# Zero matmuls in TensorE's idle stretches at the start, all of batch 1 transposed on TensorE, and load limits in the kernel's own schedule

## The chip, the cores and the metric

The kernel runs on one core of a Trainium2 chip. The metric is device time in microseconds (us), the median of several executions of the whole program. The page of the profile is one execution, so its span differs a little from the median. PE is TensorE, DVE is VectorE, ACT is ScalarE, POOL is GpSimd and SP is SyncE. POOL starts nearly all loads. SP starts the first loads of q and k, the DMA transposes and the stores.

For one core, "slow" means that the run was more than 1.5% above the fastest of the same kernel. Ratios below use fast runs alone; medians and ranges are of all runs.

## The reference

Block-sparse attention feeds a linear "multiplicative" feed-forward layer (FFN). There are 4 batches of 8 heads, 768 positions and 64 dimensions per head.

```python
scores = q @ k.T / 8                               # per head
mask   = near | first block | last block | 3 sampled blocks per block of 32
attn   = softmax(where(mask, scores, -1e9)) @ v
x      = attn.transpose(0, 2, 1, 3).reshape(3072, 512)
out    = ((x @ w1) * (x @ w2)) @ w3 @ w_out        # 512 -> 1024 -> 1024 -> 512
```

## The kernel before

The kernel is a list of tasks, each with an estimated cost on each engine that may do it. A list scheduler inside the kernel simulates the five engines, decides the order, and emits the instructions in that order. Each engine then runs its own list strictly in that order. So a number in the simulation does not change any instruction. It changes who stands before whom, and an engine that meets an input that has not landed stands still, with everything behind it.

The parts that matter here are these (`...` marks cuts):

```python
PRM = dict(..., trb=6, ..., warm=0.0, nat=4, big=10)    # trb: pairs of heads transposed by PE

# Plan.run, the list scheduler
free.update({"PE": 0.9, "ACT": 2.1, "DVE": 0.9, "POOL": 1.25, "SP": 0.75})
...
if self.spare and free["PE"] < PRM["warm"]:             # warm = 0.0: never true
    ...                                                 # would insert one zero matmul
...
if t.kind == "load":
    from_ = max(lane, t.end + 1.75)
    lane = from_ + t.bytes / 375e3
    t.seen = lane + 0.2                                 # when the data is thought to land
elif t.kind == "xbar":                                  # DMA transposes
    ...
    t.seen = t.end + 1.6 + more
...
# one pair of heads: q and k have to be turned into head_dim x positions
if (b, pr) in by_pe:            # the first trb pairs: 12 PE transposes each for q and k, one PSUM copy each
    m = add("tr ...", {PE: 0.35 + SWITCH}, tr, deps=[LD[src], t_ident], ...)
    add("tc ...", both(0.81, 0.56), ...)                # ACT or DVE
else:                           # the others: DVE reorders into a "qs" buffer (4 of them), SP transposes by DMA
    m = add("re ...", {DVE: 0.37}, ..., writes=[("qs", b, pr, x)], ...)
    add("xb ...", {SP: 1.25}, dma_start(..., transpose=True), reads=[("qs", b, pr, x)], kind="xbar")
...
# attention output xn -> x, the FFN's input: also a DMA transpose on SP's queue
add("xx ...", {SP: 1.25}, dma_start(out=x, in_=xn, transpose=True), kind="xbar")
```

Batch 0 has four pairs and batch 1 has four. So `trb=6` sends the last two pairs of batch 1, and all of batches 2 and 3, through DVE and the DMA transposes.

The softmax here doesn't subtract the row's maximum and nothing guards it: scores larger than these inputs give would overflow.

Of the kernel before, what the change touches and what calls it, by code (L numbers as in the profile page):

```python
# [9 lines left out]
BF16 = mybir.dt.bfloat16  # L10
# [5 lines left out]
SEEN = {"PE": 0.22, "ACT": 0.10, "DVE": 0.10, "POOL": 0.12, "SP": 0.05}  # L16
# [6 lines left out]


PRM = dict(bias=0.4, bmask0=1.0, bmask=1.0, btc=0.5, near=0.12, soon=0.06, kprio=2.0, eprio=0.5, aprio=1.0,
           hprio=1.0, vprio=1.5, w3prio=10.0, ebufs=4, both=0.25, fo="31", pcopy=4.0, trb=6, units="tttt",
           warm=0.0, nat=4, big=10)
LONG = ("load", "xbar", "store")


# [10 lines left out]
class Plan:  # L41
# [12 lines left out]
    def add(self, name, costs, go, deps=(), writes=(), reads=(), kind="", prio=0, mode="N", flight=0.0, bias=None):  # L54
        t = Task(name, costs, [d for d in deps if d is not None], list(writes), list(reads), go,
                 kind, prio, mode, flight)
        t.bias = {"DVE": PRM["bias"]} if bias is None else bias
        for key in set(t.writes) | set(t.reads):
            self.users[key] += 1
        self.tasks.append(t)  # L60
        return t
# [32 lines left out]
    def run(self):  # L94
        waiting = {id(t): len(t.deps) for t in self.tasks}
        after = defaultdict(list)
        for t in self.tasks:
            for d in t.deps:
                after[id(d)].append(t)
        ready = [t for t in self.tasks if not waiting[id(t)]]  # L100
        free = defaultdict(float)
        free.update({"PE": 0.9, "ACT": 2.1, "DVE": 0.9, "POOL": 1.25, "SP": 0.75})
        lane = 0.0
        lanes = []
        mode = "N"
        self.log = []
        n = 0
        while ready:
            best = None
            ests = defaultdict(list)  # L110
            for t in ready:
                b = self.buffer_ready(t)
                if b is None:
                    continue
                base = b
                for eng in t.costs:
                    at = base
                    for d in t.deps:
                        at = max(at, d.end if d.eng == eng and not d.flight and d.kind not in LONG else d.seen)
                    t.base[eng] = max(at, free[eng])  # L120
                eng = min(t.costs, key=lambda e: t.base[e] + t.costs[e] + t.bias.get(e, 0.0))
                ests[eng].append((t.base[eng], t))
            if not ests:
                raise RuntimeError("stuck: " + " ".join(t.name for t in ready[:40]))
            picks = []
            for eng, cands in ests.items():
                if eng == "PE":
                    p = self.pick_pe(cands, free, mode)
                else:
                    p = self.pick(eng, cands, free)  # L130
                if p:
                    picks.append((p[0], eng, p[1]))
            if self.spare and free["PE"] < PRM["warm"]:
                pe = min([p[0] for p in picks if p[1] == "PE"], default=1e9)
                rest = min([p[0] for p in picks if p[1] != "PE"], default=1e9)
                if pe > free["PE"] + 0.2 and rest > free["PE"]:
                    w = self.spare(mode)
                    w.start, w.end, w.eng = free["PE"], free["PE"] + w.costs["PE"], "PE"
                    free["PE"] = w.end
                    self.log.append(w)  # L140
                    continue
            elif self.spare:
                self.spare = None
                self.left[("f", "warm")] = 0
                self.freed[("f", "warm")] = free["PE"] + SEEN["PE"]
            picks.sort(key=lambda p: (p[0], p[1]))
            start, eng, t = picks[0]
            if eng == "PE":
                if t.mode != mode:
                    start = max(start, free["PE"] + SWITCH)  # L150
                mode = t.mode
            self.commit(t, eng, start)
            free[eng] = t.end
            if t.kind == "load":
                from_ = max(lane, t.end + 1.75)
                lane = from_ + t.bytes / 375e3
                lanes.append((from_, lane, t.row))
                t.seen = lane + 0.2
                for key in t.writes:
                    self.freed[key] = t.seen  # L160
            elif t.kind == "xbar":
                busy = [row for a, z, row in lanes if a < t.start + 1.25 <= z]
                more = 4.0 * max(busy) / 4096 if busy else 0.0
                t.end = t.start + 1.25 + more
                free[eng] = t.end
                t.seen = t.end + 1.6 + more
                for key in set(t.writes) | set(t.reads):
                    self.freed[key] = max(self.freed[key], t.seen)
            elif t.kind == "store":
                for key in set(t.writes) | set(t.reads):  # L170
                    self.freed[key] = max(self.freed[key], t.end + 3.0)
            self.log.append(t)
            ready.remove(t)
            for u in after[id(t)]:
                waiting[id(u)] -= 1
                if not waiting[id(u)]:
                    ready.append(u)
            n += 1
        if n != len(self.tasks):
            raise RuntimeError("left over: " + " ".join(t.name for t in self.tasks if t.end is None)[:400])  # L180
        order = sorted(range(n), key=lambda i: (self.log[i].start, i))
        return self.log
# [35 lines left out]
def kernel(  # L218
# [12 lines left out]
    nc = tc.nc  # L231
# [12 lines left out]
    PE, ACT, DVE, POOL, SP = "PE", "ACT", "DVE", "POOL", "SP"  # L244
    both = lambda a, d: {ACT: a, DVE: d}
# [29 lines left out]
    def fixed(name, shape, dt):  # L275
        return const.tile(shape, dt, tag=name, name=name)
# [3 lines left out]
    def T(*key, shape=None, dt=None):  # L280
        if key[0] == "v1":
            return v1_all[:, (key[1] * NP + key[2]) % 8]
        if key not in tl:
            sh, ty, _, _ = spec[key[0]]
            tl[key] = pools[key[0]].tile(shape or sh, dt or ty, tag=key[0], name=key[0])
        return tl[key]

    plan = Plan({name: s[2] for name, s in spec.items()})
    add = plan.add
# [38 lines left out]
    def load(name, out_of, src, nbytes, writes, deps=()):  # L328
        seq[0] += 1
        t = add(name, {POOL: 0.73}, lambda t: nc.gpsimd.dma_start(out=out_of(), in_=src),  # L330
                deps=deps, writes=writes, kind="load", prio=seq[0])
        t.bytes = nbytes
        t.row = 1536 if name.startswith("ld") else 4096
        return t

# [8 lines left out]
    for nm, dst, src, at in (("qn", q32, qv, 4.0), ("kn", k32, kv, 5.0)):  # L344
        ld = add(f"first {nm}", {SP: 0.43}, lambda t, dst=dst, src=src: nc.sync.dma_start(
            out=dst, in_=src[0][:, 0:2]), prio=-2, flight=at - 1.2)
# [31 lines left out]
    for item in LOADS.split():  # L378
        kind, rest = item[0], item[1:]
# [8 lines left out]

    t_ones = add("ones", {DVE: 0.15}, lambda t: nc.vector.memset(
        v1_all[:, :, :, :, D:].rearrange("p a b c d -> p (a b c) d"), 1.0), prio=-1)  # L390
    zero = fixed("zero", [128, 512], BF16)
    t_zero = add("zero", {DVE: 0.2}, lambda t: nc.vector.memset(zero, 0.0), prio=-1)
    add("warm", {PE: 0.43}, lambda t: nc.tensor.matmul(
        T("f", "warm"), lhsT=zero[:, :128], rhs=zero, start=True, stop=True),
        deps=[t_zero], writes=[("f", "warm")], prio=-1)
    plan.users[("f", "warm")] += 1

    def spare(mode):
        rows = 64 if mode == "S" else 128
        return Task("spare", {PE: 0.11}, (), (), (), lambda t: nc.tensor.matmul(  # L400
            T("f", "warm")[:, :256], lhsT=zero[:rows, :128], rhs=zero[:rows, :256], start=True, stop=True),
            "spare", 0, mode, 0.0)
    plan.spare = spare

    def dve(name, cost, deps, go, **kw):
# [30 lines left out]
    for i, (lo, n) in enumerate(((0, 512), (512, 256))):  # L436
# [3 lines left out]
            deps=[t_Ab, t_hot], writes=[key], prio=2)  # L440
# [67 lines left out]
    units = []  # L508
# [11 lines left out]
    for m in range(len(tiles) // 2):  # L520
        ek = ("e", m)
        exps, masks = [], []
        for j, (b, t3, pr, kp) in enumerate(tiles[2 * m:2 * m + 2]):
            sk, qk = ("s", b, t3, pr, kp), ("qkt", b, pr)

            def sc(t, sk=sk, qk=qk, t3=t3, kp=kp):
# [12 lines left out]
                prio=PRM["eprio"]))  # L539
# [3 lines left out]
            deps=exps + [t_mask[t3, kp], t_mask[t3, kp + 1]], writes=[ek], prio=PRM["kprio"])  # L543
        for j, (b, t3, pr, kp) in enumerate(tiles[2 * m:2 * m + 2]):
# [14 lines left out]
            if kp < 2:  # L559
# [7 lines left out]
                deps=[tr], reads=[ok, rk], writes=[xk], prio=0)  # L567
# [4 lines left out]
    for b in range(B):  # L572
        for t3 in range(NT):
            xk = ("xn", b, t3)
            i, half = divmod(b * NT + t3, 2)
            for qt in range(2):
# [3 lines left out]
                    deps=Xdone[b, t3], writes=[("x", i)], reads=[xk], kind="xbar", prio=0)  # L580
# [33 lines left out]
    for i in range(NU):  # L614
        hk, xk = [("big", "h", i, j) for j in range(NF // 2)], ("x", i)
        hs = []
        for f in range(NF):
            ends = {}
            for which, w in (("w1", w1_sb), ("w2", w2_sb)):
                key = ("f", which, i, f)  # L620
                last = None
                for part in range(2):
                    def mm(t, key=key, w=w, f=f, part=part, xk=xk):
                        for c in range(2 * part, 2 * part + 2):
# [4 lines left out]
                               writes=[key], reads=[xk],  # L629
# [66 lines left out]
```

## Time and profile before

The median was 262.42 us in 3 runs (260.9 to 263.03).

| what | value | read from |
|---|---|---|
| span of the profiled run | 261.6 us | page |
| PE busy | 242.8 us, 93% | page, part 1 |
| first real PE work | 4.60 us | timeline |
| PE at half rate | until about 22.9 us | durations in the timeline |
| PE idle in 60-70 and 80-90 us | 2.9 and 3.2 us | windows |
| last value product (end of attention) | 222.4 us | groups by source line |

The profiled run itself took 263.41 us, a little more than the three, at a mean clock of 0.987.

The first view is the page: busy microseconds by engine, then the granted PE clock in 40 slices (tenths of full speed).

```profile
PE 242.8 (93%) x2555; PEld 128.5 (49%) x2597; DVE 175.2 (67%) x305; ACT 186.6 (71%) x231; POOL 44.6 (17%) x73
...
PEclk9999999998899979999999999999999999999999
```

PE is the limit. The clock row says "full speed" from the start, but the durations say otherwise. The next lines are the timeline of the opening: start, duration, engine, line of the kernel, operation, output<-inputs, shape and count, and in brackets the idle time before and what ended it. L477 is the transposes of q and k, L531 the scores.

```profile
4.60 0.85 PE L477 MATMUL f<-ident,qn 128*64 128x128 bf16 x12 [2.39 <-ACT qn L292]
8.59 1.03 PE L531 MATMUL s<-qkt 64*128 64x256 bf16 x8
...
20.22 0.54 POOL L330 DMA_DIRECT2D big<-in_moe_w_dram  x1 [1.65 <-DMA kn<-in_k_dram]
22.20 0.84 PE L477 MATMUL f<-ident,kn 128*64 128x128 bf16 x12 [0.36 <-issue]
23.94 0.61 PE L531 MATMUL s<-qkt 64*128 64x256 bf16 x8
```

The same eight score matmuls take 1.03 us at 8.59 and 0.61 us at 23.94, so the clock was at half at first and the row did not record it. The Trainium skill describes this in "TensorE: Matmul & The Clock Gate", Part 1: the array starts at half its clock and is released only after about 3.4 us of sustained activity. The durations agree with the start at half. POOL's wait at 20.22 shows when k of pair 2 landed (about 19.9 us), so that pair's scores could not have come much earlier whatever PE did.

The second loss is two stalls at 61 and 87 us. L625 is x times w1 or w2, L541 the mask product, L486 DVE's reorder into a `qs` buffer, L489 the DMA transposes of q and k, L554 the value products.

```profile
63.57 0.38 PE L625 MATMUL f<-x,w 128*128 128x512 bf16 x1 [2.22 <-DMA x<-xn]
...
73.31 16.99 SPq L489 DMA_TRANSPOSE qkt<-qs  x6
83.08 1.22 DVE L541 TENSOR_TENSOR e<-e,mask 128x2048 bf16<-128x2048 bf16 x1
88.40 0.36 DVE L486 COPY qs<-qn 128x768 bf16<-128x768 bf16 x1 [4.10 <-DMA vn<-in_v_dram]
...
89.96 0.41 PE L554 MATMUL o<-v,e 128*128 128x65 bf16 x8 [3.14 <-DVE xn L564]
```

At 63.57 PE had waited 2.22 us for a DMA transpose of x. At 88.40 DVE had stood for 4.10 us, and PE, which needed DVE's xn, for 3.14 us. The windows view shows what the stalls cost: busy microseconds (and instruction counts) of each engine in each stretch, then the clock, the DMA share and GB/s.

```profile
60.00:70.00 10.00, 7.09 (x78) 3.76 (x80) 5.52 (x11) 5.16 (x7) 1.00 (x2) 0.83 1.02 96
70.00:80.00 10.00, 9.94 (x106) 5.04 (x106) 8.91 (x16) 8.32 (x11) 2.90 (x5) 1.00 1.30 161
80.00:90.00 10.00, 6.81 (x67) 3.16 (x64) 5.40 (x14) 7.35 (x9) 4.99 (x7) 1.00 1.20 142
90.00:100.00 10.00, 9.61 (x92) 4.74 (x95) 7.90 (x14) 4.75 (x6) 2.15 (x3) 0.83 1.49 190
```

PE's busy column is 7.09 and 6.81 where its neighbours have 9.6 to 9.9, and the clock drops to 0.83 after each stall. A mean of 0.83 over 10 us is about 3.4 us at half, a loss of 1.7 us each.

### The profile page before, as it was taken

How to read it: one execution, taken by the hardware profiler on the slowest of the kernel's cores; microseconds unless marked ns; L12 is line 12 of the kernel's file. 1: busy time of each engine (PE TensorE's matmuls, PEld its weight loads, DVE VectorE, ACT ScalarE, POOL GpSimd, SP SyncE). 2: the span in 40 equal slices, each digit the busy share in tenths (PEclk: the TensorE clock that was granted, in tenths of full speed). 3: DMA queues.
4: the chain of work that ended last, by engine and by line, in shares of the span. 5: the costliest groups of instructions: out<-in, count | busy, mean ns of one | idle time of the engine just before them, and what ended most of it. 6: DMA issues, size and time to landing. Idle time of an engine off the chain costs nothing.

```text
span 261.6 us, 6156 instructions
## 1 busy us (share of the span) xinstructions
PE 242.8 (93%) x2555; PEld 128.5 (49%) x2597; DVE 175.2 (67%) x305; ACT 186.6 (71%) x231; POOL 44.6 (17%) x73
## 2 busy tenths in 40 slices
PE   3999999995999499999999999999999999999994
PEld 1565556652454245554555554554545545444441
DVE  6774688896687467789886767767677667412420
ACT  4683688995777548998979998798987986324331
POOL 9544455532136123000000000000000000000000
PEclk9999999998899979999999999999999999999999
DMA  7999999999599999676332202023020240213013
GB/s 177 175 207 205 209 210 197 198 160 146 77 156 124 190 195 179 125 136 171 73 98 74 62 4 40 29 75 102 3 41 3 63 140 3 40 49 114 1 40 120
DMA packets 48993, 28.85 MB, mean 110 GB/s; under 512 B 30533, under 2 KB 43845, under 8 KB 48965
## 3 DMA queue, kind: packets, MB, share of 16 engines
q0 software_dynamic: 15872, 14.29, 37.7%
q1 hardware_dynamic: 33092, 14.16, 25.8%
q8 instruction: 20, 0.33, 0.5%
q14 instruction: 9, 0.07, 0.1%
HBM read 29.36 MB, written 6.29 MB: 136 GB/s over the span
## 4 chain that ended last, share of the span: by engine, by line
PE 63%; DMA 18%; issue 11%; POOL 6%; DVE 1%; ACT 0%; POOLq 0%
PE f L625 27%; PE f L645 16%; PE o L554 10%; PE s L531 10%; DMA vn<-in_v_dram 6%; DMA kn<-in_k_dram 5%; DMA w<-in_moe_w_dram 4%; DMA big<-in_moe_w_dram 3%; POOL qn L330 2%; POOL kn L330 2%; POOL vn L330 1%; POOL wo L330 1%; DVE e L541 0%; POOL big L330 0%; POOL hotf L354 0%
## 5 line engine op out<-in xcount | busy, mean ns | idle before, releaser
L537 ACT ACTIVATE e<-s 128x1024 bf16<-128x1024 f32 x144 | 139.7, 1025 | 23.3 <-PE s L531 23.1
L625 PE MATMUL f<-x,w 128*128 128x512 bf16 x361 | 91.4, 382 | 4.0 <-DMA x<-xn 2.2
L541 DVE TENSOR_TENSOR e<-e,mask 128x2048 bf16<-128x2048 bf16 x72 | 87.4, 1218 | 10.3 <-ACT e L537 10.0
L554 PEld LDWEIGHTS <-e 128*128 128x128 bf16 x1152 | 45.7, 99 | 26.0 <-DVE xn L564 8.3
L554 PE MATMUL o<-v,e 128*128 128x65 bf16 x1152 | 52.2, 197 | 3.5 <-DVE xn L564 3.1
L636 DVE TENSOR_TENSOR big<-f,a 128x512 bf16<-128x512 f32 x48 | 33.1, 689 | 30.1 <-PE f L625 23.7
L625 PEld LDWEIGHTS <-w 128*128 128x128 bf16 x384 | 32.6, 98 | 36.7 <-issue 8.2
L531 PE MATMUL s<-qkt 64*128 64x256 bf16 x576 | 47.1, 281 | 1.3 <-ACT e L537 1.1
L645 PE MATMUL f<-wf,big 128*128 128x512 bf16 x180 | 46.4, 385 | 1.0 <-issue 0.5
L633 ACT CAST a<-f 128x512 bf16<-128x512 f32 x48 | 28.2, 588 | 26.4 <-PE f L625 26.4
L531 PEld LDWEIGHTS <-qkt 64*128 64x128 bf16 x576 | 22.7, 96 | 31.6 <-issue 26.9
L645 PEld LDWEIGHTS <-big 128*128 128x128 bf16 x192 | 16.3, 98 | 18.0 <-issue 4.1
L562 DVE RECIPROCAL rec<-o 128x4 f32<-128x4 f32 x48 | 8.6, 179 | 19.7 <-PE o L554 19.2
L292 ACT COPY ob<-f 128x512 f32<-128x512 f32 x20 | 11.7, 586 | 14.0 <-PE f L645 12.9
L564 DVE TENSOR_TENSOR xn<-o,rec 128x256 bf16<-128x256 f32 x48 | 20.4, 424 | 1.7
L606 PE MATMUL f<-wo,w3t 128*128 128x512 bf16 x57 | 16.2, 384 | 0.6 <-issue 0.3
L330 POOL DMA_DIRECT2D kn<-in_k_dram x15 | 10.8, 719 | 21.8 <-DVE qs L486 11.2
L330 POOL DMA_DIRECT2D qn<-in_q_dram x15 | 10.8, 723 | 15.2 <-DVE qs L486 9.6
L330 POOL DMA_DIRECT2D vn<-in_v_dram x16 | 11.5, 716 | 10.2 <-DVE v L499 5.4
L292 DVE COPY qkt<-f 128x768 bf16<-128x768 bf16 x9 | 5.0, 555 | 3.6 <-PE f L477 3.6
L606 PEld LDWEIGHTS <-w3t 128*128 128x128 bf16 x64 | 4.9, 98 | 4.6 <-issue 1.6
L477 PE MATMUL f<-ident,qn 128*64 128x128 bf16 x72 | 4.1, 268 | 2.4 <-ACT qn L292 2.4
(54 smaller groups left out, 85.8 us busy)
## 6 DMA issues: line engine op xcount, KB each, us to landing
out_dram<-ob SPq DMA_DIRECT2D x24, 256.0 KB, 2.0
vn<-in_v_dram POOLq DMA_DIRECT2D x16, 192.0 KB, 6.7
qn<-in_q_dram POOLq DMA_DIRECT2D x15, 192.0 KB, 7.5
kn<-in_k_dram POOLq DMA_DIRECT2D x15, 192.0 KB, 7.4
big<-in_moe_w_dram POOLq DMA_DIRECT2D x8, 256.0 KB, 9.2
w<-in_moe_w_dram POOLq DMA_DIRECT2D x8, 256.0 KB, 9.7
wo<-in_moe_w_out_dram POOLq DMA_DIRECT2D x2, 512.0 KB, 8.8
q<-in_q_dram SPq DMA_DIRECT2D x1, 384.0 KB, 2.9
```

Of the source, the lines that this page charges most:

```text
L292: (nc.scalar.copy if t.eng == ACT else nc.vector.tensor_copy)(out, in_)
L330: t = add(name, {POOL: 0.73}, lambda t: nc.gpsimd.dma_start(out=out_of(), in_=src), deps=deps, writes=writes, kind="load", prio=seq[0])
L531: nc.tensor.matmul(s[:, h, k2 * QT:(k2 + 1) * QT], lhsT=z[64 * h:64 * h + 64, 1, kc * 128:(kc + 1) * 128], rhs=z[64 * h:64 * h + 64, 0, t3 ...
L537: exps.append(add(f"E {m} {j}", {ACT: 0.97}, lambda t, sk=sk, ek=ek, j=j: nc.scalar.activation(T(*ek)[:, j], T(*sk), AF.Exp, scale=1.0 / 8 ...
L541: tm = add(f"K {m}", {DVE: 1.23}, lambda t, ek=ek, t3=t3, kp=kp: nc.vector.tensor_tensor(T(*ek), T(*ek), mask[:, t3, kp:kp + 2, :].unsquee ...
L554: nc.tensor.matmul(o[:, qt, h, :], lhsT=e[:, j, h, lo:lo + 128], rhs=w[:, h, kc, :], start=kc == 0 and qt == 0 and h == 0, stop=kc == C - ...
L564: tx = add(f"xn {rk}", {DVE: 0.42}, lambda t, rk=rk, ok=ok, xk=xk, pr=pr: nc.vector.tensor_tensor(T(*xk)[:, :, 128 * pr:128 * pr + 128].re ...
L606: nc.tensor.matmul(T(*key), lhsT=T("w3t", i)[:, j, :], rhs=wo_sb[:, j, :], start=j == 0, stop=j == NF - 1)
L625: nc.tensor.matmul(T(*key), lhsT=w[:, c, f * 128:(f + 1) * 128], rhs=T(*xk)[:, c, :], start=c == 0, stop=c == 3)
L633: ta = add(f"a {i}{f}", {ACT: 0.58}, lambda t, ak=ak, key=ends["w1"][0]: nc.scalar.copy(T(*ak), T(*key)), deps=[ends["w1"][1]], reads=[end ...
L636: nc.vector.tensor_tensor(T(*hk)[:, 512 * (f % 2):512 * (f % 2) + 512], T(*key), T(*ak), op=ALU.mult),
L645: nc.tensor.matmul(T(*key), lhsT=T(*hk[f // 2])[:, 512 * (f % 2) + n * 128:512 * (f % 2) + (n + 1) * 128], rhs=wf_sb[:, f, :], start=f == ...
```

## The change

It has three parts:

- **Zeros.** Wherever the simulated PE would idle before the first value product, a 256-column matmul of zeros is inserted. It writes into the PSUM bank that the first value product will clear anyway.
- **Transposes.** `trb` goes from 6 to 8, so PE turns q and k for all of batch 1.
- **Load limits.** The simulation allows only 8 loads in flight, thinks that they land 0.3 us later (3.0 us later for q, k and v of batches 1 to 3), and that DMA transposes land 1.0 us later.

```diff
-... trb=6, units="tttt", warm=0.0, nat=4, big=10)
+... trb=8, units="tttt", nat=4, big=10)
-free.update({"PE": 0.9, ...})
+free.update({"PE": 1.5, ...})
-if self.spare and free["PE"] < PRM["warm"]:
+if self.spare:
-    if pe > free["PE"] + 0.2 and rest > free["PE"]:
+    if pe > free["PE"] + 0.12 and rest > free["PE"] - 0.1:
         w = self.spare(mode)                  # one zero matmul
+if t.kind == "value":
+    self.spare = None                         # no more zeros from the first value product on
 if t.kind == "load":
+    if len(lanes) >= 8:
+        t.end = max(t.end, lanes[-8][1] + 0.3)
+        free[eng] = t.end
-    t.seen = lane + 0.2
+    t.seen = lane + 0.2 + t.slack             # slack 3.0 for q, k, v of batches 1-3, else 0.3
-    t.seen = t.end + 1.6 + more               # DMA transposes
+    t.seen = t.end + 2.6 + more
-add("warm", ..., one 512-column zero matmul into an "f" bank)
 def spare(mode):
-    ... T("f", "warm")[:, :256] ...
+    ... T("o", 0, 0, 0) ... [:, :256] ...
```

In the built program there are 45 zero matmuls, 31 of them in one block before the first transpose. There are 48 more transposes and 4 more PSUM copies for them, 4 fewer DVE reorders and 4 fewer DMA transposes, and the rest of the work is the same in another order.

More of the change, by code (lines that the diff above doesn't have):

```diff
@@ L25 @@
 PRM = dict(bias=0.4, bmask0=1.0, bmask=1.0, btc=0.5, near=0.12, soon=0.06, kprio=2.0, eprio=0.5, aprio=1.0,
-           hprio=1.0, vprio=1.5, w3prio=10.0, ebufs=4, both=0.25, fo="31", pcopy=4.0, trb=6, units="tttt",
-           warm=0.0, nat=4, big=10)
+           hprio=1.0, vprio=1.5, w3prio=10.0, ebufs=4, both=0.25, fo="31", pcopy=4.0, trb=8, units="tttt",
+           nat=4, big=10)
 LONG = ("load", "xbar", "store")
@@ L101, in run @@
         free = defaultdict(float)
-        free.update({"PE": 0.9, "ACT": 2.1, "DVE": 0.9, "POOL": 1.25, "SP": 0.75})
+        free.update({"PE": 1.5, "ACT": 2.1, "DVE": 0.9, "POOL": 1.25, "SP": 0.75})
         lane = 0.0
@@ L141, in run @@
                     continue
-            elif self.spare:
-                self.spare = None
-                self.left[("f", "warm")] = 0
-                self.freed[("f", "warm")] = free["PE"] + SEEN["PE"]
             picks.sort(key=lambda p: (p[0], p[1]))
             start, eng, t = picks[0]
+            if t.kind == "value":
+                self.spare = None
             if eng == "PE":
@@ L332, in load @@
         t.bytes = nbytes
+        t.slack = 3.0 if name.startswith("ld") and writes[0][1] > 0 else 0.3
         t.row = 1536 if name.startswith("ld") else 4096
@@ L390 @@
         v1_all[:, :, :, :, D:].rearrange("p a b c d -> p (a b c) d"), 1.0), prio=-1)
-    zero = fixed("zero", [128, 512], BF16)
+    zero = fixed("zero", [128, 256], BF16)
     t_zero = add("zero", {DVE: 0.2}, lambda t: nc.vector.memset(zero, 0.0), prio=-1)
-    add("warm", {PE: 0.43}, lambda t: nc.tensor.matmul(
-        T("f", "warm"), lhsT=zero[:, :128], rhs=zero, start=True, stop=True),
-        deps=[t_zero], writes=[("f", "warm")], prio=-1)
-    plan.users[("f", "warm")] += 1
     def spare(mode):
@@ L400, in spare @@
         return Task("spare", {PE: 0.11}, (), (), (), lambda t: nc.tensor.matmul(
-            T("f", "warm")[:, :256], lhsT=zero[:rows, :128], rhs=zero[:rows, :256], start=True, stop=True),
-            "spare", 0, mode, 0.0)
+            T("o", 0, 0, 0).rearrange("p t h d -> p (t h d)")[:, :256], lhsT=zero[:rows, :128],
+            rhs=zero[:rows, :256], start=True, stop=True), "spare", 0, mode, 0.0)
     plan.spare = spare
```

## The prediction

> **What bounds the kernel now.** TensorE: the page's busy table gives PE 93% of 261.6 us, ACT 71%, DVE 67%; the last 35 us are PE alone. The time is PE's streaming work, plus slow clock, plus PE's idle stretches. From the timeline, four losses:
> 1. No real work before 4.60 us (the cast of q).
> 2. From 4.6 to about 22.9 us PE runs at half rate although the clock row says full: eight score matmuls take 1.03 us at 8.59 and 0.61 at 30.12. I estimate 15 us of streaming there that would take 7.6. This agrees with the Trainium skill, "TensorE: Matmul & The Clock Gate", Part 1: the clock starts at half and is released after about 3.4 us of sustained activity.
> 3. 61.3 to 63.5: PE waits 2.2 us for a DMA transpose of x that took up to 9.9 us to land among the loads.
> 4. 86.8 to 90.0: PE waits 3.1 us for DVE's xn; DVE had sat 4.1 us waiting for a late v load. After 3 and 4 the granted clock of 60-70 and 90-100 falls to 0.83, about 1.7 us each.
>
> **What the change does.** The order has 31 zero matmuls before the first transpose, then 14 in gaps up to the first value product. At the cold rate (0.215 us each, as the mask products show) 31 take 6.6 us; with release on the way I estimate they end at 6.2 to 8.2 us, so real work starts about 2 us later. Batch 1's last two pairs go through PE: 48 more transposes, about 2 us of PE, four PSUM copies (0.56 us DVE or 0.81 ACT) for four DVE reorders (0.35), and four DMA transposes fewer in the congested stretch. The schedule's load limits only reorder: FFN of unit 0 starts after all of batch 1's transposes, giving x more time to land.
>
> **How much is critical.** Cold loss: at most 7.6 us, minus 2 for the later start. But k of pair 2 landed only at about 19.9 us (the queue's wait at 20.22 shows it) and was turned at 22.2; a warm PE will wait for it. So I expect about 2.5 us from the opening. From 30 to 60 us ACT and DVE are near 90% too; no more is gained there, and the extra transposes cost up to 2. Stalls 3 and 4 with their slow clock are worth up to 9.6 us; I expect a good half to go. From unit 0's first second-layer product (91.9 us now) the remaining work is the same; I expect that point at 85 to 87.
>
> **Prediction.** 254.5 us, range 248.5 to 260. Faster by over 2%: 0.68; within 2%: 0.28; slower: 0.04.
>
> **What would show it.**
> - Timeline: zeros from about 1.6 us; q's first transposes at 6.2 to 8.2 us taking 0.53, scores 0.61 from the start.
> - First score group of pair 2 at about 21.5 (now 23.94), after a PE wait for k.
> - Windows: 60-70 and 80-100 at clock 1.00, PE idle there under 2 us in place of 6.5.
> - PE's tail of FFN alone lengthens to about 40 us (the order has less FFN done by the last value product).
> - Exponentials unchanged, 1.03 us.
>
> **What would make it wrong.** The zeros never release the clock, or it falls back in gaps: then the later start is pure loss. New waits, as q and k loads of batch 1 now gate PE's in-order queue near 50-58 us, or late values of batch 2 block DVE again: then 259 or more. If both stalls vanish and none comes: about 249.

## The result, and the profile after

The median after is 254.4 us (254.23 to 254.47, 4 runs) against 262.73 us before (260.9 to 264.15, 4 runs). The ratio is 0.9686, with a 95% interval of 0.9625 to 0.9747. In later rounds (e5 below) it was 0.9737 (0.969 to 0.9783). A ratio is the mean time of one kernel's fast runs over that of the other's fast runs of the same rounds, so it is not quite the ratio of the medians.

The page after has PE at 240.6 us of 252.7:

```profile
PE 240.6 (95%) x2647; PEld 130.5 (52%) x2689; DVE 174.9 (69%) x305; ACT 186.4 (74%) x231; POOL 44.9 (18%) x73
```

The timeline after follows. Line numbers moved: L397 is the zeros, L474 the transposes, L528 the scores, L622 x times w1 or w2, L642 the second FFN layer.

```profile
1.47 5.41 PE L397 MATMUL o<-zero 128*128 128x256 bf16 x31 [1.47 <-DVE zero L394]
6.81 0.53 PE L474 MATMUL f<-ident,qn 128*64 128x128 bf16 x12
...
9.89 0.61 PE L528 MATMUL s<-qkt 64*128 64x256 bf16 x8
...
20.49 0.53 PE L474 MATMUL f<-ident,kn 128*64 128x128 bf16 x12
21.91 0.61 PE L528 MATMUL s<-qkt 64*128 64x256 bf16 x8
...
61.72 1.02 PE L622 MATMUL f<-x,w 128*128 128x512 bf16 x3 [0.90 <-DMA x<-xn]
...
85.78 0.59 PE L642 MATMUL f<-wf,big 128*128 128x512 bf16 x2
```

The 31 zeros take 5.41 us, and after them, in this opening, every group of 12 transposes takes 0.53 us and every group of eight scores 0.61 us. Real work starts 2.2 us later (6.81 against 4.60), yet pair 2's scores come 2.0 us earlier (21.91 against 23.94). The wait for x is 0.90 us instead of 2.22. The first second-layer product starts at 85.78 us instead of 91.93.

The windows view after, in the same stretches:

```profile
60.00:70.00 10.00, 9.00 (x108) 4.88 (x109) 8.04 (x16) 8.43 (x11) 3.95 (x6) 1.00 1.37 169
70.00:80.00 10.00, 9.78 (x121) 5.43 (x121) 9.24 (x17) 9.01 (x12) 2.15 (x3) 1.00 1.12 142
80.00:90.00 10.00, 9.89 (x120) 5.20 (x121) 8.62 (x17) 8.83 (x12) 2.86 (x4) 1.00 0.93 118
90.00:100.00 10.00, 9.79 (x122) 5.39 (x122) 8.54 (x17) 8.90 (x11) 3.57 (x5) 1.00 1.32 167
```

PE idles 1.5 us in these 40 us (40 less the sum of its column) where it idled 6.6, and the clock stays at 1.00.

### The profile page after: what moved, and what is told of

Read it like the earlier page. It is cut to its first block, busy times and chain, and to the rows that moved or that the text cites. A ratio compares the mean times of both kernels' runs of the same rounds, so it can differ in the third digit from the quotient of the medians.

```text
span 252.7 us, 6330 instructions
## 1 busy us (share of the span) xinstructions
PE 240.6 (95%) x2647; PEld 130.5 (52%) x2689; DVE 174.9 (69%) x305; ACT 186.4 (74%) x231; POOL 44.9 (18%) x73
## 4 chain that ended last, share of the span: by engine, by line
PE 86%; DVE 4%; DMA 4%; ACT 3%; issue 2%; SPq 0%
PE f L622 33%; PE f L642 17%; PE s L528 14%; PE o L551 14%; PE f L603 5%; DMA x<-xn 4%; PE o L397 2%; DVE e L538 2%; ACT e L534 2%; PE f L474 1%; PE f L591 1%; DVE xn L561 1%; ACT qkt L293 0%; DVE w3t L293 0%; SPq L574 0%
## 5 line engine op out<-in xcount | busy, mean ns | idle before, releaser
L622 PE MATMUL f<-x,w 128*128 128x512 bf16 x359 | 90.4, 379 | 2.8 <-issue 1.0
L551 PEld LDWEIGHTS <-e 128*128 128x128 bf16 x1152 | 44.1, 97 | 22.9 <-DVE xn L561 6.5
L551 PE MATMUL o<-v,e 128*128 128x65 bf16 x1152 | 50.6, 194 | 0.8 <-DVE xn L561 0.4
L622 PEld LDWEIGHTS <-w 128*128 128x128 bf16 x384 | 32.4, 98 | 35.3 <-issue 6.7
L642 PE MATMUL f<-wf,big 128*128 128x512 bf16 x183 | 46.2, 380 | 0.9 <-issue 0.6
L528 PE MATMUL s<-qkt 64*128 64x256 bf16 x576 | 45.2, 272 | 0.7 <-ACT e L534 0.7
L528 PEld LDWEIGHTS <-qkt 64*128 64x128 bf16 x576 | 22.2, 94 | 27.5 <-issue 24.1
L642 PEld LDWEIGHTS <-big 128*128 128x128 bf16 x192 | 16.1, 98 | 17.3 <-issue 3.2
L397 PE MATMUL o<-zero 128*128 128x256 bf16 (+1 forms) x45 | 7.8, 331 | 1.5 <-DVE zero L394 1.5
L293 DVE COPY qkt<-f 128x768 bf16<-128x768 bf16 x13 | 7.1, 552 | 2.0 <-PE f L474 1.9
## 6 DMA issues: line engine op xcount, KB each, us to landing
out_dram<-ob SPq DMA_DIRECT2D x24, 256.0 KB, 2.0
big<-in_moe_w_dram POOLq DMA_DIRECT2D x8, 256.0 KB, 8.9
w<-in_moe_w_dram POOLq DMA_DIRECT2D x8, 256.0 KB, 9.7
```

The costliest lines, as they stand in the source:

```text
L293: (nc.scalar.copy if t.eng == ACT else nc.vector.tensor_copy)(out, in_)
L528: nc.tensor.matmul(s[:, h, k2 * QT:(k2 + 1) * QT], lhsT=z[64 * h:64 * h + 64, 1, kc * 128:(kc + 1) * 128], rhs=z[64 * h:64 * h + 64, 0, t3 ...
L551: nc.tensor.matmul(o[:, qt, h, :], lhsT=e[:, j, h, lo:lo + 128], rhs=w[:, h, kc, :], start=kc == 0 and qt == 0 and h == 0, stop=kc == C - ...
L622: nc.tensor.matmul(T(*key), lhsT=w[:, c, f * 128:(f + 1) * 128], rhs=T(*xk)[:, c, :], start=c == 0, stop=c == 3)
L642: nc.tensor.matmul(T(*key), lhsT=T(*hk[f // 2])[:, 512 * (f % 2) + n * 128:512 * (f % 2) + (n + 1) * 128], rhs=wf_sb[:, f, :], start=f == ...
```

## The experiments

The main question was how the gain splits between the opening and the stalls, and which of the three parts removes the stalls. The zeros hardly touch the order of the other instructions, because the simulation assumes a full clock either way. So the three parts can be switched independently, and six kernels fill the cube between before and after. The other two parts do change the order: with `trb=8` or with the limits alone the sequence on DVE is another one than before, with the zeros alone it is the same. Every kernel below gave the right result.

### e1 to e4: one part at a time

The edits, against the kernel before:

```diff
 e1  all of the zeros' lines; not trb, not the load limits
 e2  trb=8 and the load limits; not the zeros
 e3  trb=8 alone
 e4  the load limits alone
```

> The 45 zero matmuls alone; the instruction order of everything else and the batch-1 transposes as in the kernel before. Theory A (the opening gives about 2.5 us because k of pair 2 lands near 20 us whatever PE does, and most of the gain is the two stalls): 259 to 261 us, scores 0.61 from the start, first score group of pair 2 near 22, both stalls (2.2 us before the first x,w matmul, 3.1 us near 87) still there with a clock below 1.00 after them. Theory B (a warm start is the whole gain, the stalls only followed from a late PE): 254 to 256 us, stalls gone.

> Eight pairs turned on PE and the load limits in the schedule, but no zero matmuls: the order is that of the kernel after without its zeros. Theory A: about 257 us, PE at half rate to near 22 us, no stall over 1 us at 60 and at 87. Theory B: 261 us or more.

> Only batch 1's last two pairs on PE. If the transposes through the DMA queues cause the stalls (theory A1): 257 to 259 us, both stalls short. If the load limits are what moves producer and consumer apart (A2): 261 to 264, at least one stall of 2 us left, and 2 us more PE work.

> Only the schedule's load limits and later landings. A2: 257 to 259 us, both stalls short. A1: 261 to 263 us, a stall of 2 us or more left near 60 or 87, as batch 1's pairs still go through the DMA transposes.

| run | zeros | trb=8 | limits | median us | ratio to before (95%) |
|---|---|---|---|---|---|
| e1 | yes | | | 259.6 | 0.9943 (0.985 to 1.0036) |
| e2 | | yes | yes | 256.55 | 0.984 (0.9783 to 0.9896) |
| e3 | | yes | | 257.56 | 0.9883 (0.981 to 0.9956) |
| e4 | | | yes | 265.58 | 1.02 (1.011 to 1.029) |

Theory A holds. The zeros alone bring nothing that is clear of noise (the interval includes 1), and both stalls are still in their trace, as these lines of PE's waits in e1 show (waiter, releaser, us in total, times, longest):

```profile
PE o L548 <- DVE xn L558: 2.9, 1, 2.9
PE f L619 <- DMA x<-xn: 1.5, 1, 1.5
```

Without the zeros (e2) most of the gain is there, and no wait of PE is longer than 0.5 us once its real work has begun. Theory B, that a warm start is the whole gain, falls. In e3, with the transposes alone, the waits that are left of the two stalls are short:

```profile
PE f L625 <- DMA x<-xn: 1.2, 1, 1.2
DVE qs L486 <- DMA qkt<-qs: 0.7, 2, 0.5
```

The surprise is the load limits, which alone made the kernel slower (265.58 us, outside both ranges that were expected). I had expected them to be able to remove the stalls by themselves. The next lines are the chief waits of DVE and of PE in e4, then its windows.

```profile
DVE qs L490 <- DMA qkt<-qs: 8.1, 3, 3.4
...
PE o L558 <- DVE xn L568: 4.7, 3, 3.6
...
100.00:110.00 10.00, 7.10 (x72) 4.26 (x73) 6.14 (x11) 4.90 (x5) 0.00 (x0) 0.50 0.91 164
```

Here the profile names the releaser plainly. DVE's reorder of q and k (L490) stood 8.1 us until a DMA transpose had emptied one of the four `qs` buffers. Because DVE runs in order, the mask products and xn behind it stood too, PE waited for those, and the clock fell to 0.50 in 100-110 us.

e3 showed something else. It has no zeros, yet in its profiled run the clock was released near 10.5 us and fell back again before 17 us. L554 is the value products; eight of them take 0.41 us at the full rate. The last line is from its windows view.

```profile
8.69 1.03 PE L531 MATMUL s<-qkt 64*128 64x256 bf16 x8
10.98 0.39 PE L531 MATMUL s<-qkt 64*128 64x256 bf16 x4
16.47 0.62 PE L554 MATMUL o<-v,e 128*128 128x65 bf16 x8
19.40 0.85 PE L477 MATMUL f<-ident,qn 128*64 128x128 bf16 x12
...
15.00:20.00 5.00, 4.75 (x56) 3.45 (x53) 3.73 (x9) 3.35 (x7) 2.03 (x4) 0.50 1.23 204
```

So without zeros the time of the release differs from run to run. The profiled run of e3 took 256.21 us and its other three 257.43 to 258.84. Its mean clock on record is 0.983, theirs 0.997 to 0.999. That the fastest run shows the lowest clock is a trap: a fall after an early release is recorded, a late first release is not (the profiled run of e2 is at half rate to about 22 us with a mean clock of 1.0).

### e5 to e8: the rest of the cube, and the front zeros alone

```diff
 e5  the kernel after, unchanged
 e6  after without the load limits
 e7  after with trb=6
 e8  after, same order, but only the first 31 zeros are emitted:
+    if t.kind == "spare":
+        zeros += 1
+        if not (zeros <= 31): continue
```

> The kernel after once more, as the yardstick on the same chip as the next three: 254 to 255 us, runs within 0.5 us of each other.

> After without the load limits and later landings in the schedule (zeros and eight pairs on PE kept). If the transposes on PE are what removes the stalls and the limits only polish: 255 to 256.5 us, one wait of 1 to 2 us left before the first x,w matmul near 60. If the limits matter as much: 258 or more.

> After without batch 1's last two pairs on PE (zeros and limits kept). The run with the limits alone was slower than before, so here too: 262 to 265 us, PE stalls between 85 and 110 with a clock of about 0.5 there. A rival (the limits were bad only because the opening was cold) says 256 or less.

> The order of the kernel after, but only the 31 zero matmuls ahead of the first transpose are issued, the 14 in the later gaps are not. If the gap fillers keep the clock up: in this kernel it falls to half rate somewhere between 9 and 20 us (scores 1.03 in place of 0.61, as the run with the transposes alone showed between 14 and 21 us), and the runs spread to 1 us or more, 255 to 256 us. If the front alone does it: 254 to 254.8 and narrow.

| run | zeros | trb=8 | limits | median us | range | ratio to before (95%) |
|---|---|---|---|---|---|---|
| e5 (after) | yes | yes | yes | 254.66 | 254.38 to 256.88 | 0.9737 (0.969 to 0.9783) |
| e6 | yes | yes | | 255.71 | 253.73 to 260.31 | 0.9731 (0.9671 to 0.9791) |
| e7 | yes | | yes | 266.26 | 265.38 to 267.45 | 1.0176 (1.0127 to 1.0224) |
| e8 | 31 of 45 | yes | yes | 255.01 | 254.55 to 256.08 | 0.9747 (0.9705 to 0.9788) |

The part `trb=8` is the one that removes the stalls. Taking it out of the kernel after (e7) costs 11.6 us (266.26 less 254.66) and turns the gain into a loss, a little more than expected. In e7 DVE stood 9.1 us behind the DMA transposes, in 6 waits, and the rival that blamed the cold opening of e4 falls. These are that wait and a stretch of e7's windows:

```profile
DVE qs L483 <- DMA qkt<-qs: 9.1, 6, 2.9
...
100.00:110.00 10.00, 9.31 (x104) 5.61 (x104) 5.67 (x8) 6.44 (x8) 0.00 (x0) 0.56 0.61 136
```

The load limits make no difference to the fast runs: 0.9731 without and 0.9737 with them. Two of e6's six runs were slow (259.06 and 260.31) and none of e5's. Two in six against none in six is too few to call the limits a protection, and the profile of e6 is one of the two slow ones. It does have both stalls again (PE waits 2.2 us for x and 2.4 us for xn), so `trb=8` without the limits may not remove them in every run. Over all runs, 8 of the 51 of kernels without the limits are slow and none of the 46 with them. Most of the 51 are of the kernel before, and no run was made to test this, so a protection is suggested and not shown. The yardstick e5 missed its own expectation (runs within 0.5 us): one run of six took 256.88 us.

e8 expected the clock to fall back without the gap fillers, and it did: the mean clock on record is 0.987 to 0.993 in all six of its runs, and 0.99 to 1.0 in those of e5. These are its timeline and its windows:

```profile
14.57 0.66 PE L551 MATMUL o<-v,e 128*128 128x65 bf16 x16
18.41 1.06 PE L551 MATMUL o<-v,e 128*128 128x65 bf16 x16
20.25 0.85 PE L474 MATMUL f<-ident,qn 128*64 128x128 bf16 x12
24.36 0.61 PE L528 MATMUL s<-qkt 64*128 64x256 bf16 x8
...
63.11 1.03 PE L622 MATMUL f<-x,w 128*128 128x512 bf16 x4
...
15.00:20.00 5.00, 4.28 (x53) 3.07 (x50) 4.03 (x9) 3.24 (x7) 2.00 (x3) 0.62 1.24 205
```

Sixteen value products go from 0.66 to 1.06 us between 14.57 and 18.41, and pair 2's scores are back at 24.36 us, no earlier than in the kernel before. Yet the median is only 0.35 us above that of after, which is not clear of noise, and the profiled run is one of the two slowest of e8: its span is 254.1 us against 252.7. So 2.45 us of lead at 22 us (24.36 less 21.91) are at most 1.4 us at the end. Most of where it goes can be seen: the kernel after waits 0.90 us for x at 61.7, and e8 shows no such wait. At that first product of x the lead is down to 1.4 us (63.11 less 61.72). x comes by its own path, which a faster opening of PE does not shorten as much.

### e9 and e10: the size of the opening

```diff
 e9   the kernel of e2 (no zeros) again, for the same chip and rounds as e10
 e10  after, same order, with 20 zeros at the front and the 14 fillers:
+    if not (zeros <= 20 or zeros > 31): continue
```

> The kernel without zeros once more, now on one chip and in the same rounds as the kernel with zeros that follows, to size the opening. Theory A: 256.5 to 257, that is 2 to 2.5 us above the next one, and a wider spread, since the clock is released at another time in each run.

> After, with 20 zero matmuls at the front in place of 31 (the 14 gap fillers kept). Release came after about 18 zeros in the profiled run, so q's transposes should start near 5.6 to 6 us in place of 6.8, but k of pair 2 still lands near 20: 254 to 254.7, no gain clear of noise. If the start of PE's work is what counts: 253.5. If 20 are too few to be sure of the release: a spread over 1 us and 255 or more.

e9 took 256.0 us (254.49 to 256.28), ratio 0.9757 (0.9714 to 0.9801). e10 took 254.29 us (253.8 to 254.72), ratio 0.9701 (0.9661 to 0.9741). On the same chip, then, the zeros are worth about 1.7 us (256.0 less 254.29). The 2 to 2.5 us that I expected is a little too much. The spread of e9 came out as expected: one run of six was at 254.49, the others at 255.7 to 256.3. That one has a mean clock of 0.986 on record and the others 1.0, as in e3. The same kernel had the ratio 0.984 as e2, on another chip, so small differences of ratios from different chips mean little here.

The timeline of e10 tests the claim that a load gates pair 2:

```profile
5.85 0.71 PE L474 MATMUL f<-ident,qn 128*64 128x128 bf16 x12
...
18.21 0.62 PE L591 MATMUL f<-ident,big 128*128 128x128 bf16 x8 [0.37 <-DMA big<-in_moe_w_dram]
19.18 0.53 PE L474 MATMUL f<-ident,qn 128*64 128x128 bf16 x12 [0.35 <-DMA qn<-in_q_dram]
20.61 0.53 PE L474 MATMUL f<-ident,kn 128*64 128x128 bf16 x12
22.04 0.61 PE L528 MATMUL s<-qkt 64*128 64x256 bf16 x8
```

PE starts real work 1.0 us earlier than in after (5.85 against 6.81), and pair 2's k is turned at 20.61 against 20.49: the lead is gone by then. PE had stood 0.37 us for a load of a weight before 18.21 and 0.35 us for a load of q before 19.18. So loads do gate this stretch, but it is not k that PE waits for. e10 is not told apart from the kernel after. It is as fast as any version here and beats the kernel before, but it is not a new best.

### e11 and e12: what DVE stood for at 84 us

My prediction said that DVE stood for a late load of v, as the trace names it. e4 and e7 suggested a buffer. So I doubled the `qs` buffers and left the order of all instructions as it was (the simulation still counts four):

```diff
 e11  the kernel before        e12  the kernel of e4 (limits alone), both with:
-  tc.tile_pool(name="p_" + name, bufs=n, **kw)
+  tc.tile_pool(name="p_" + name, bufs=8 if name == "qs" else n, **kw)
```

> The kernel before in the same order, but with eight buffers in place of four for the reordered q and k that the DMA transposes read. If the 4 us stop of DVE near 84 is a wait for a buffer that a slow DMA transpose still holds (theory S): that stop and PE's 3.1 us wait near 87 go, 256 to 259 us. If it is a wait for a late load (theory V, my reading in the prediction): they stay within 1 us, 260 to 262 us.

> The limits-only kernel (265.6 us) with the same eight buffers. Theory S: the 8 us that DVE stood behind DMA transposes there are gone, and with them the clock of 0.5 at 100 to 110; 257 to 260 us. Theory V: 264 to 266.

e11 took 265.26 us, ratio 1.0112 (1.0052 to 1.0172). e12 took 261.82 us, ratio 0.9994 (0.9927 to 1.006). Neither theory got its time for e11. DVE's 4.1 us stop is gone: no wait for a DMA by a `qs` copy is left in its list, and the reorder that stood until 88.40 ran at 82.43 us. So the stop was a buffer held by a slow DMA transpose, and not a late load. But the time got worse by 1.1%, and the next lines show a new wait: e11's timeline, then PE's waits.

```profile
89.49 5.18 SPq L577 DMA_TRANSPOSE x<-xn  x2
94.76 9.99 SPq L489 DMA_TRANSPOSE qkt<-qs  x4
103.07 0.61 PE L625 MATMUL f<-x,w 128*128 128x512 bf16 x1 [4.40 <-DMA x<-xn]
...
PE f L625 <- DMA x<-xn: 5.9, 2, 4.4
```

PE now waits for x instead, 5.9 us in two waits, 4.4 of it until 103 us. The two transposes of x were issued from 89.49 us on, and the trace gives 11.6 us from issue to landing for the first. The buffers moved the wait from DVE to PE's own input. Both are waits for a DMA transpose that lands late. In e12 the buffers did bring back 3.8 us (265.58 less 261.82, on two chips), about half of what theory S asked for, and there too PE was left with a wait of 4.0 us for x.

This fits that, of the three parts, only `trb=8` removed the stalls: it is the one part that takes work away from that queue. But it also gives a new order, and no run had the one without the other. The traces do not show a quicker queue: in 75-95 us the kernel before issues five DMA transposes of q and k, which take 8.5 us to land in the median, and the kernel after six, which take 7.9. What is gone there is the waiting for them. So whether the lighter queue or the order did it stays open.

Why the DMA transposes are slow just there I did not isolate. In the kernel before, those of x took 2.5 us to land in the median and 9.9 at most, and the slow ones are early, while the loads run. The last load starts at 101.12 us. The transposes issued after 110 us took 2.5 us (x) and 2.8 us (q and k) in the median, 4.4 at most. The Trainium skill, "DMA: Bandwidth & Descriptors", section "Issuing engines are not separate DMA queues", says that transfers started from SP and from POOL run on the same 16 DMA engines and interleave. These numbers fit that. But after 110 us fewer transposes are under way as well, and no run here took the loads alone away.

## Why the prediction was right

The prediction was 254.5 us and the result 254.4. Its steps fared as follows.

1. **Zeros release the clock, q's transposes at 6.2 to 8.2 us, scores 0.61 from the start.** Right: 6.81 us and 0.61.
2. **Pair 2 is gated by a load; the first scores of pair 2 at about 21.5; 2.5 us from the opening.** The scores came at 21.91. e10 confirms a gate, but of loads of q and of a weight: no wait for k itself is listed before 20.49 in the kernel after, as I had said there would be. The size was 1.7 us (e9 against e10), not 2.5. The term that I left out is that a lead at 22 us is partly spent on a later wait for x: in the profiled runs of e9 and e10 it is 2.4 us at pair 2's scores (24.42 less 22.04) and 1.3 us at the first product of x (63.16 less 61.88), where e10 waits 0.94 us and e9 does not.
3. **A good half of the 9.6 us in the two stalls goes.** More went: 5.0 us of the 6.6 us of PE idle time in 60-100 us (38.46 less 33.45, the sums of PE's column), and both falls of the clock. With 1.7 us for each fall that is 8.4 of the 9.6. Add 1.7 us for the opening, take off 2.1 for the extra transposes (step 4), and the sum is 8.0 us, an estimate, of the 8.9 by which the two spans differ. The prediction's "about 249", for both stalls gone and no new one, counts the whole opening as well (7.6 less 2), and that did not come.
4. **The extra transposes cost up to 2 us.** Not measured by itself. Four groups of twelve at 0.53 us are 2.1 us, an estimate. e3 shows the net: with them and without zeros or limits, 0.9883.
5. **First second-layer product at 85 to 87, the remaining work the same.** It came at 85.78, 6.15 us earlier than before. The span shrank by 8.9 us (261.6 less 252.7), so 2.8 us more were gained after that point. The stretch 90-100 us, with its clock of 0.83 before, lies there; the prediction counted that loss among the stalls but put this point ahead of it.
6. **The tail of FFN alone lengthens.** Right: the last value product is at 208.1 us in place of 222.4, while the span fell by only 8.9, so the tail grew by 5.4 us, from 39.2 to 44.6. (The prediction counted 35 us before, from another point, so its "about 40" is a growth of about 5.)

The exponentials stayed at 1.03 us, as said. That the total came within 0.1 us is luck: the opening was put 0.8 us too high, more of the stalls went than "a good half", and the median of the kernel before itself lay between 260.66 and 262.87 from round to round. Two of its reasons were wrong in ways that the total hides. It read "DVE had sat 4.1 us waiting for a late v load", and e11 shows a `qs` buffer held by a DMA transpose. And it gave the load limits a large part in the removal of the stalls, by the order that they make ("FFN of unit 0 starts after all of batch 1's transposes, giving x more time to land"), with the four fewer DMA transposes only as an aside. The cube shows that `trb=8` alone does most of it, that the limits alone cost 2%, and that with `trb=8` the limits change nothing that the fast runs show.

## What to carry to other kernels

When in-order engines wait on one another, find the queue that is slow at the far end and try to take work off it. Here, moving four DMA transposes to the busiest engine paid (with the new order that this brought), while deeper buffers in the kernel before and a more careful schedule only moved the wait. Trust durations over the clock row and the mean clock until the first release, and expect a faster opening to be worth less at the end than it is at its own end. Where a trace names a load as the releaser of a wait that also needs a free buffer, change the buffer count with the order fixed before believing it.

## What the Trainium skill lacked or had wrong

- "TensorE: Matmul & The Clock Gate", section "Why this matters for your kernels", asks for no PE gaps above about 3 us to avoid a drop. In e8 the clock fell back between 14.6 and 18.4 us although no PE gap in 13 to 20 us was longer than 0.52 us; in e3 it fell back likewise. The page elsewhere says that short idles between groups of matmuls can make the clock oscillate, but gives no length for them.
- The same page, Part 1, gives about 3.4 us of sustained matmuls to the release. In the kernel before PE was busy for 9.89 us of 10-20 us, and the clock stayed at half to about 22.9. Matmuls of zeros did release it. 31 of them took 5.41 us in the profiled run of after; from 0.215 us each at half rate and 0.108 at full, with 0.17 us for the end of the group, I estimate the release after about 18 of them, 3.9 us after the first. In the five profiled fast runs with 31 zeros they took 5.04 to 6.44 us (q's transposes start at 6.44 to 7.84), so by the same estimate the release came after 14 to 27 zeros, 3.1 to 5.9 us after the first.
- The same page warns that clock events in a trace can be unreliable, but not how they fail here: the row shows 1.00 from the start to 22.9 us in the kernel before, although groups took 1.03 in place of 0.61 us. Falls after the first release are recorded (0.50 in e3's 15-20 us).
- "DMA: Bandwidth & Descriptors" has no time for DMA transposes beside running loads. Here those of x took 2.5 us to land in the median and up to 9.9, and six of q and k held SP's queue for 16.99 us. With the loads over (issued after 110 us) the medians are 2.5 us for x and 2.8 us for q and k.
